# Attention and a gated two-layer network on one core: q and k of 33 head pairs turned by DMA instead of TensorE

## The chip, the core and the metric

One Trainium2 chip, one of its eight cores. The core has five engines that run side by side, each with its own queue of instructions in program order: TensorE (PE, matrix multiplications; its weight loads are shown apart as PEld), VectorE (DVE), ScalarE (ACT), GpSimd (POOL) and SyncE (SP, which here issues nearly all DMAs and does nothing else). 16 DMA engines move data between the memory of the chip (DRAM) and the core's two on-chip memories, SBUF and, for the results of TensorE, PSUM; a DMA can't reach PSUM. The metric is the time of one execution on the device, in microseconds (us).

## What is computed

```python
# q, k, v: (8, 12, 448, 64): batch, heads, sequence, head size
scale = 1.0 / np.sqrt(q.shape[-1])
scores = scale * np.matmul(q, k.transpose(0, 1, 3, 2))
m = np.max(scores, axis=-1, keepdims=True)
e = np.exp(scores - m)
attn = e / (np.sum(e, axis=-1, keepdims=True) + np.exp(-m) + 1e-09)
attn_out = np.matmul(attn, v)
x = attn_out.transpose(0, 2, 1, 3).reshape(3584, 768)
h = x @ w_in                       # (768, 2048)
g = h * np.tanh(softplus(h))       # "mish"
out = g @ w_out                    # (2048, 768)
```

Inputs and output are float32; the kernel multiplies in bfloat16.

## The kernel before, in words

The 96 heads are taken as 48 pairs, numbered by batch and then by head, six pairs a batch. A pair's two heads lie side by side on the 128 partitions. The sequence of 448 is split as 112 rows of 4.

For a pair, the steps are these. `load_pair` (L121) loads q, k and v by SP. `cast_pair` and `cast_v` (L165, L185) turn them into bfloat16 on POOL: `q_bf`, `k_bf`, `v_bf`. `transpose_pair` (L190) turns q and k on TensorE, eight transposes of 112 x 128, four for each, into a PSUM bank each (two halves of an `sc` tile in the repeating part). `evac_qk` (L221) brings them to SBUF: VectorE scales q and lays it out in `qd`, a tile with zeros in such places that one multiplication by the pair's k serves both heads (two instructions, L254, one for each head); ScalarE copies k into `kT` (L262). `scores` (L291) multiplies (L311) into one of three `sc` tiles of two PSUM banks and VectorE takes the negated row maximum (L332). `exps` (L337) has ScalarE raise the scores into `en` and sum the rows (L345). `denominators` (L363) and `normalise` (L410) have VectorE divide (seven instructions on a pair, L414) and SP turn the pair's 128 x 3584 numbers by one DMA transpose, `en` to `eT` (L422). `av_pair` (L445) multiplies by v (L462), and VectorE copies the result into `xT` (L475), the input of the network. `mm1_mish` (L493) is the first layer for 128 of the 2048 columns: six multiplications (L498), then ScalarE's Mish (L504). `mm2_part` (L523) is the second layer in small chunks (L551), with a copy by VectorE (L534) and a store by SP (L516).

The order is written out by hand. After a head part for the first batch (pairs 0 to 5), the loop at L653 runs over units of three pairs. A unit has two stretches:

- Twelve steps (L664), four for a pair: the exponentials of one step, some chunks of the second layer for an earlier batch (spread by the weights at L589), scores two steps ahead. At steps 0, 3 and 6 (`LOAD_AT`) the loads, the casts of the pair loaded one time before, and the cast of a v are issued. The pair whose cast is issued at these steps belongs to the next unit.
- Eight groups of the first layer (L724), for a batch whose attention is complete. Beside the first group stand the denominators of the unit's three pairs and the first normalisation; after groups 1, 3 and 5 the transposes and the evacuation of the next unit's three pairs; from group 4 on the first scores of the next unit.

Buffers are taken from pools in turn: `bf` with 4 tiles for each of q_bf and k_bf and 12 for v_bf, `qk` with 3 for kT. A tile that is taken again waits until its last reader is done. A DMA is also held until the DMA eight issues before it has landed, as the eight semaphores for them are used in turn.

Of the kernel before, what the change touches and what calls it, by code (L numbers as in the profile page):

```python
# [10 lines left out]
BF16 = mybir.dt.bfloat16  # L11
# [4 lines left out]
UNIT_PAIRS = 3  # L16
# [3 lines left out]
def kernel(  # L20
# [9 lines left out]
    nc = tc.nc  # L30

    B, H, S, D = q.shape
# [3 lines left out]
    NT = 4  # L36
    SP_ = S // NT
    HP = H // 2
# [9 lines left out]
    N_PAIRS = B * HP  # L48
# [4 lines left out]
    def pool(name, bufs, space=None):  # L53
        if space is None:
            return ctx.enter_context(tc.tile_pool(name=name, bufs=bufs))
        return ctx.enter_context(tc.tile_pool(name=name, bufs=bufs, space=space))
# [1 line left out]
    PS = bass.MemoryType.PSUM  # L58
    singles = pool("singles", 1)
    ld_pool = pool("ld", 3)  # L60
    bf_pool = pool("bf", 4)
    qk_pool = pool("qk", 3)
    st_pool = pool("st", 5)
    hl_pool = pool("hl", 4)
    rb_pool = pool("rb", 2)
# [38 lines left out]
    loaded, casted, qkT, att, xT, o_sbs, stats = {}, {}, {}, {}, {}, {}, {}  # L104
# [60 lines left out]
    def cast_pair(p, with_v=True):  # L165
        if p >= N_PAIRS:
            return
        q_f, k_f, v_f = (loaded[p].get(nm) for nm in "qkv")
        q_bf = bf_pool.tile([SP_, NT, 2, D], BF16, tag="q_bf", name="q_bf")
        k_bf = bf_pool.tile([SP_, NT, 2, D], BF16, tag="k_bf", name="k_bf")  # L170
        v_bf = bf_pool.tile([SP_, 2, NT * D], BF16, tag="v_bf", name="v_bf", bufs=12)
        by_t = "p h (t d) -> p t h d"
        q_t, k_t = (t.rearrange(by_t, t=NT) for t in (q_f, k_f))
        if p == 0:
            nc.vector.tensor_copy(out=k_bf, in_=k_t)
            for half in (slice(0, NT // 2), slice(NT // 2, NT)):
                nc.vector.tensor_copy(out=q_bf[:, half], in_=q_t[:, half])
        else:
            nc.gpsimd.tensor_copy(out=q_bf, in_=q_t)  # L179
            nc.gpsimd.tensor_copy(out=k_bf, in_=k_t)  # L180
        casted[p] = (q_bf, k_bf, v_bf)
        if with_v:
            cast_v(p)

    def cast_v(p):  # L185
        if p >= N_PAIRS:
            return
        nc.gpsimd.tensor_copy(out=casted[p][2], in_=loaded.pop(p)["v"])  # L188

    def transpose_pair(p, bank=None):  # L190
        if p >= N_PAIRS:
            return
        q_bf, k_bf, _ = casted[p]
        if bank is None:
            ps = mo_take()
            ps_k = mo_take() if p == 0 else ps
        else:
            ps, ps_k = sc_tiles[2 - bank][:, 0, :], sc_tiles[2 - bank][:, 1, :]
        by_s = [
            t[:, :].bitcast(BF16).rearrange("p (s n) -> p s n", s=2)[:, s, :]  # L200
            for s, t in enumerate((ps, ps_k))
        ]
        by_2 = sc_tiles[2][:, 0, :].bitcast(BF16)
        srcs = list(enumerate((q_bf, k_bf)))
        for s, src in reversed(srcs) if p == 0 else srcs:
            for t in range(NT):
                to = by_2 if p == 0 and s == 0 and t >= NT // 2 else by_s[s]
                nc.tensor.transpose(  # L208
                    to[:, t * SP_ : (t + 1) * SP_],
                    src[:, t].rearrange("p h d -> p (h d)"),  # L210
                    ident[:SP_, :SP_],
                )
        own = [] if bank is not None else [ps, ps_k] if p == 0 else [ps]
        qkT[p] = (by_s, own)
# [6 lines left out]
    def evac_qk(p, act=False):  # L221
        if p >= N_PAIRS:
            return
        (q_ps, k_ps), own = qkT[p]
        mo_free.extend(own)
        q_reads = []
        qd = q_diag[p % 3]
        kT = qk_pool.tile([128, S], BF16, tag="kT", name="kT")
        if p < DIAG_FROM:
            qT = qd.rearrange("d i h r -> d (i h r)")[:, 0:S]  # L230
            qkT[p] = (qT, kT)
            if p == 0:
                nc.scalar.copy(kT, k_ps[:, 0:S])
                by_2 = sc_tiles[2][:, 0, :].bitcast(BF16)
                for ps, half in (q_ps, slice(0, S // 2)), (by_2, slice(S // 2, S)):
                    nc.vector.tensor_scalar(
                        out=qT[:, half], in0=ps[:, half], scalar1=SCALE, scalar2=None,
                        op0=ALU.mult,
                    )
                return  # L240
            if act:
                nc.scalar.mul(qT, q_ps[:, 0:S], SCALE)
            else:
                q_reads.append(nc.vector.tensor_scalar(
                    out=qT, in0=q_ps[:, 0:S], scalar1=SCALE, scalar2=None, op0=ALU.mult
                ))
        else:
            qkT[p] = (qd, kT)
            if p < DIAG_FROM + 3:
                nc.vector.memset(qd[0:64, :, 1, :], 0.0)  # L250
                nc.vector.memset(qd[64:128, :, 0, :], 0.0)
            for h in range(2):
                rows = slice(64 * h, 64 * h + 64)
                q_reads.append(nc.vector.tensor_scalar(  # L254
                    out=qd[rows, :, h, :],
                    in0=q_ps[rows, 0:S].rearrange("d (i r) -> d i r", i=QB),
                    scalar1=SCALE, scalar2=None, op0=ALU.mult,
                ))
        if own and not act:
            nc.vector.tensor_copy(out=kT, in_=k_ps[:, 0:S])  # L260
        else:
            k_read = nc.scalar.copy(kT, k_ps[:, 0:S])  # L262
            if not own:
                apart(k_read, *q_reads)
# [145 lines left out]
    def normalise(p, dma=True):  # L410
# [9 lines left out]
        if dma:  # L420
            n = NT - 1 if p < HEAD else NT
            nc.sync.dma_start_transpose(  # L422
# [168 lines left out]
    LEAD = UNIT_PAIRS + 1  # L591
    LOAD_AT = (0, 3, 6)
    HEAD = HP

    BY_PE = {HEAD - 1: 1, HEAD: -2, HEAD + 1: 2}
    AV_AT = {0: {1: 3, 5: 4, 8: 5}, 1: {1: 8, 4: 6, 8: 7}}
# [20 lines left out]

    for p in range(HEAD):
        for s in range(STEPS):
# [33 lines left out]
    for u in range(UNITS_PER_B, N_UNITS + 2 * UNITS_PER_B):  # L653
# [10 lines left out]
        for n in range(steps):  # L664
            pi, s = divmod(n, STEPS)
            p, idx = p0 + pi, p0 * STEPS + n
            late_tp = u == UNITS_PER_B and n == STEPS
            exps(idx)
            if u == UNITS_PER_B + 1 and n == 0:
                for j in range(2):  # L670
                    turn_on_pe(HEAD, j, busy_first=3)
            flush_late()
            if late_tp:
                transpose_pair(p0 + 2)
                evac_qk(p0 + 2)
            if held and n == 1:
                late.extend(held)
                held.clear()
                flush_late()
            late.extend(slow)  # L680
            slow.clear()
            acc += weight[n]
            want = int(total * acc / sum(weight) + 1e-6)
            while done < want:
                fn, w = filler.popleft()
                fn()
                done += w
            scores_ahead(end)
            if n in LOAD_AT:
                at = p0 + LOAD_AT.index(n)  # L690
                load_pair(at + LEAD, "qk")
                load_pair(at + 1, "v")
                cast_pair(at + LEAD - 1, with_v=False)
                cast_v(at)
            for pe, n0 in BY_PE.items():
                j = n - n0
                first = 2 if pe == HEAD else 0
                if pe // UNIT_PAIRS == u - 1 < first_mm2 - 1 and first <= j < NT:
                    turn_on_pe(pe, j, busy_first=1)
            spread = RDEN_AT.get(u - UNITS_PER_B, {})  # L700
            if n in spread:
                on_act = u < first_mm2
                spread_rden(
                    spread[n], copy=nc.scalar.copy if on_act else nc.vector.tensor_copy,
                    behind=slow if on_act else late,
                )
            early = AV_AT.get(u - UNITS_PER_B)
            if early is not None and n == 7:
                keep_busy(6, bank=mo_free[0])
            if early is not None:  # L710
                if n in early:
                    av_pair(early[n], half=p)
            elif s == (2 if pi else 0) and N_PAIRS <= p < N_PAIRS + UNIT_PAIRS:
                av_pair(p - UNIT_PAIRS)
            if u - UNITS_PER_B < len(W_AT):
                at = (u - UNITS_PER_B, n)
                load_w(W_AT[at[0]].get(n, 0), behind=W_BEHIND.get(at))
# [6 lines left out]
        for f in range(FF_U):  # L724
# [19 lines left out]
            if f in (3, FF_U - 1) and p0 >= LATE_DIV:  # L744
                p = todo[1 + f // (FF_U - 1)]
# [33 lines left out]
```

## Time and profile before

| | |
|---|---|
| Time, three runs | 480.35 us in the median (479.74 to 483.63) |
| The profiled execution | 479.66 us, its span 477.9 us |
| Granted TensorE clock | 0.996 |
| Busy: PE, PEld | 458.8 us, 257.8 us |
| Busy: DVE, ACT, POOL | 358.7, 344.7, 103.8 us |
| L208, the transposes of q and k: spans of one | 213 ns, pipelined |
| L254, q scaled and laid out: 72 of them | 27.7 us, 385 ns each |
| L262, kT copied by ScalarE: 39 of them | 20.8 us, 534 ns each |
| L179 and L180, casts of q and k on POOL | 635 and 622 ns each |
| L422, DMA transposes of en: 45 of them | 6.7 us from issue to landing, in the median |
| A load of q or k, 224 KB | 5.2 us from issue to landing, in the median |

The profile is of one execution, made by the hardware's profiler. Busy time of PE counts pipelined multiplications whose spans overlap, so that the sum of single spans is more than the busy time. Times in the views are counted from the span's start. In rows of work the columns are the engine, the line of the kernel, the operation, the tile written and the tiles read, their shapes and a count. An idle time of an engine is put down to what released it, by the semaphores. SPq and POOLq are the queues that issue DMAs; the length of such a row is the time for which its engine was occupied by the issue, and the data move beside and after it. The share of the DMA engines can be more than 1, since packets that overlap on one engine are counted each.

### The profile page before, as it was taken

The page shows a single profiled execution, that of the slowest core. Times are in us where ns is not written, and L with a number is a line of the kernel's source. Part 1 is how long each engine was busy: PE and PEld are TensorE (multiplying, and loading weights), DVE is VectorE, ACT ScalarE, POOL GpSimd, SP SyncE. Part 2 cuts the span into 40 slices and gives each one's busy share as a digit, 9 for nine tenths or more (in the row PEclk, how much of TensorE's full clock was granted, in tenths as well). Part 3 has the DMA queues.
Part 4 walks back from the last instruction along what each step waited for, and adds up shares of the span by engine and source line. Part 5 has one row for each costly group of instructions (what it writes and reads, how often), then busy time and mean ns, then how long its engine had stood idle before and what let it go on. Part 6 is the DMA issues. An engine that isn't in the chain of part 4 may idle for free.

```text
span 477.9 us, 9363 instructions
## 1 busy us (share of the span) xinstructions
PE 458.8 (96%) x3291; PEld 257.8 (54%) x3291; DVE 358.7 (75%) x715; ACT 344.7 (72%) x907; POOL 103.8 (22%) x186
## 2 busy tenths in 40 slices
PE   6878999999999999999999999999999999999996
PEld 3344555555555565556555555555555555556563
DVE  5899849569898998889899979888898889421011
ACT  5998878788797868788787968687887978312300
POOL 3623536106031311304040312204040300000000
PEclk9999999999999999999999999999999999999999
DMA  8999999999999979898989999989989596961122
GB/s 215 227 224 213 234 222 183 185 212 233 195 301 207 261 149 214 211 198 227 192 229 171 267 156 260 198 192 231 190 220 198 173 181 156 156 142 34 34 63 71
DMA packets 204975, 91.09 MB, mean 191 GB/s; under 512 B 161792, under 2 KB 201472, under 8 KB 204928
## 3 DMA queue, kind: packets, MB, share of 16 engines
q1 hardware_dynamic: 197408, 84.18, 81.0%
q0 software_dynamic: 7488, 6.29, 8.8%
q8 instruction: 26, 0.43, 0.4%
q14 instruction: 21, 0.17, 0.1%
q10 hardware_dynamic: 32, 0.02, 0.0%
HBM read 45.61 MB, written 11.01 MB: 118 GB/s over the span
## 4 chain that ended last, share of the span: by engine, by line
PE 69%; DVE 8%; ACT 6%; issue 1%; DVEq 0%
PE mo L498 24%; PE mo L551 24%; PE sc L311 7%; ACT en L345 6%; PE sc L462 6%; DVE negm L332 5%; PE sc L498 3%; PE sc L208 3%; DVE en L414 1%; DVE xT L475 1%; PE mo L462 1%; DVE o_sb L534 1%; PE mo L272 0%; DVE eT L437 0%; ACT L345 0%
## 5 line engine op out<-in xcount | busy, mean ns | idle before, releaser
L345 ACT ACTIVATE en<-sc,negm 128x448 bf16<-128x448 f32 x336 | 208.7, 640 | 22.5 <-DVE negm L332 20.7
L332 DVE TENSOR_REDUCE negm<-sc 128x2 f32<-128x896 f32 x192 | 182.6, 970 | 39.6 <-PE sc L311 29.3
L551 PE MATMUL mo<-w_out_sb,gT 128*128 128x384 bf16 (+1 forms) x1024 | 166.8, 307 | 0.4 <-DVE rb L402 0.4
L498 PE MATMUL mo<-xT,w_in_sb 128*128 128x448 bf16 x672 | 141.9, 353 | 0.3 <-DVE xT L475 0.3
L551 PEld LDWEIGHTS <-gT 128*128 128x128 bf16 x1024 | 96.3, 98 | 56.0 <-issue 1.9
L504 ACT ACTIVATE gT<-mo 128x448 bf16<-128x448 f32 x112 | 59.3, 543 | 78.9 <-PE mo L498 78.6
L498 PEld LDWEIGHTS <-w_in_sb 128*128 128x128 bf16 x768 | 72.7, 98 | 63.4 <-issue 3.2
L179 POOL CAST q_bf<-q_f 112x512 bf16<-112x512 f32 x47 | 29.9, 635 | 222.1 <-DMA q_f<-in_q_dram 196.1
L414 DVE TENSOR_SCALAR en<-en,rden 128x448 bf16<-128x448 bf16 x252 | 74.2, 367 | 0.8
L311 PE MATMUL sc<-kT,qd 128*128 128x448 bf16 x252 | 71.6, 354 | 0.1
L345 ACT ACTIVATION_READ_ACCUMULATOR en<-sc,negm 128x1 f32 x336 | 71.0, 211 | 0.0
L534 DVE COPY o_sb<-mo 128x384 f32<-128x384 f32 (+1 forms) x64 | 31.8, 497 | 48.3 <-PE mo L551 48.1
L462 PE MATMUL sc<-eT,v_bf 112*64 112x448 bf16 x336 | 39.8, 357 | 1.4 <-ACT en L345 0.9
L311 PEld LDWEIGHTS <-qd 128*128 128x128 bf16 x252 | 24.4, 97 | 29.0 <-issue 12.9
L188 POOL CAST v_bf<-v_f 112x512 bf16<-112x512 f32 x48 | 29.9, 624 | 31.5 <-DMA v_f<-in_v_dram 31.4
L254 DVE TENSOR_SCALAR qd<-sc 64x448 bf16<-64x448 bf16 x72 | 27.7, 385 | 6.2 <-PE sc L208 5.4
L462 PEld LDWEIGHTS <-v_bf 112*64 112x64 bf16 x384 | 20.0, 109 | 20.0 <-issue 11.6
L180 POOL CAST k_bf<-k_f 112x512 bf16<-112x512 f32 x47 | 29.2, 622 | 6.1 <-DMA k_f<-in_k_dram 3.5
L262 ACT COPY kT<-sc 128x448 bf16<-128x448 bf16 x39 | 20.8, 534 | 0.6 <-PE sc L208 0.6
L498 PE MATMUL sc<-xT,w_in_sb 128*128 128x448 bf16 x96 | 20.8, 353 | 0.0
L475 DVE CAST xT<-sc 128x448 bf16<-128x448 f32 x33 | 20.3, 614 | 0.0
L208 PEld LDWEIGHTS <-q_bf 112*128 112x128 bf16 x192 | 13.7, 99 | 10.0 <-POOL q_bf L179 2.0
(61 smaller groups left out, 278.9 us busy)
## 6 DMA issues: line engine op xcount, KB each, us to landing
k_f<-in_k_dram SPq DMA_DIRECT2D x48, 224.0 KB, 5.2
q_f<-in_q_dram SPq DMA_DIRECT2D x48, 224.0 KB, 5.2
v_f<-in_v_dram SPq DMA_DIRECT2D x48, 224.0 KB, 5.5
w_in_sb<-in_moe_w_in_dram POOLq DMA_DIRECT2D x12, 256.0 KB, 8.7
w_out_sb<-in_moe_w_out_dram POOLq DMA_DIRECT2D x8, 384.0 KB, 10.1
out_dram<-o_sb SPq DMA_DIRECT2D x7, 336.0 KB, 3.7
out_dram<-o_sb SPq DMA_DIRECT2D x8, 288.0 KB, 4.8
out_dram<-o_sb SPq DMA_DIRECT2D x8, 240.0 KB, 3.4
```

The costliest lines, as they stand in the source:

```text
L179: nc.gpsimd.tensor_copy(out=q_bf, in_=q_t)
L180: nc.gpsimd.tensor_copy(out=k_bf, in_=k_t)
L188: nc.gpsimd.tensor_copy(out=casted[p][2], in_=loaded.pop(p)["v"])
L311: nc.tensor.matmul(sc[:, bk, 0:S], lhsT=qT[:, i].rearrange("d h r -> d (h r)"), rhs=kT, start=True, stop=True,)
L332: half_max[p] = nc.vector.tensor_reduce(out=negm, in_=sc[:, 0 : len(cols), 0:S], axis=AX.X, op=ALU.max, negate=True)
L345: e = nc.scalar.activation(out=st["en"][:, :, c, 0:SP_], in_=sc[:, bk, 0:S].rearrange("q (j c) -> q j c", j=NT), func=AF.Exp, bias=st["neg ...
L414: nc.vector.tensor_scalar(out=en[:, :, i, 0:SP_], in0=en[:, :, i, 0:SP_], scalar1=st["rden"][:, i : i + 1], scalar2=None, op0=ALU.mult,)
L462: mm = nc.tensor.matmul(av[h * 64 : (h + 1) * 64, 0:S], lhsT=v_bf[:, h, j * D : (j + 1) * D], rhs=e_h, start=(j == 0), stop=(j == NT - 1),)
L498: nc.tensor.matmul(h_ps[:, 0:S], lhsT=w_in_sb[:, dm, ff * 128 : (ff + 1) * 128], rhs=xT[b][:, dm, :], start=(dm == 0), stop=(dm == DM_T - 1),)
L504: nc.scalar.activation(out=gT[:, ff, b % 2 * S : b % 2 * S + S], in_=h_ps[:, 0:S], func=AF.Mish)
L534: nc.vector.tensor_copy(out=o_sb[:, cols.start : cols.start + n_dve], in_=st["o"][:, 0:n_dve])
L551: nc.tensor.matmul(st["o"][:, 0:n_cols], lhsT=gT[:, ff, i * 128 : (i + 1) * 128], rhs=w_out_sb[:, ff, cols], start=(ff == 0), stop=(ff == ...
```

## The change

From pair 15 on (`QK_BY_DMA_FROM = 2 * HP + UNIT_PAIRS`, 33 of the 48 pairs), q and k are no longer turned by TensorE. Right behind the issue of their casts, at steps 0, 3 and 6 of the twelve, SP issues two DMA transposes for each pair, `k_bf` to `kT` and `q_bf` to a new tile `qT`. `transpose_pair` returns without work for these pairs; `evac_qk` reads `qT` from SBUF instead of PSUM for the two instructions of VectorE, and leaves out ScalarE's copy, since kT is in place. To make room, `q_bf` and `k_bf` have 3 tiles instead of 4 and `v_bf` 8 instead of 12, taken at its cast instead of at that of q and k; `kT` has 6 instead of 3, and `qT` 3.

```diff
-    bf_pool = pool("bf", 4)
-    qk_pool = pool("qk", 3)
+    bf_pool = pool("bf", 3)
+    qk_pool = pool("qk", 6)
...
+    ahead = {}
+
+    def turn_qk_by_dma(p):
+        if not QK_BY_DMA_FROM <= p < N_PAIRS:
+            return
+        kT = qk_pool.tile([128, S], BF16, tag="kT", name="kT")
+        qT = qk_pool.tile([128, S], BF16, tag="qT", name="qT", bufs=3)
+        for to, src in (kT, casted[p][1]), (qT, casted[p][0]):
+            nc.sync.dma_start_transpose(
+                out=to.rearrange("d (t p) -> d t p", t=NT),
+                in_=src.rearrange("p t h d -> p (t h d)"),
+            )
+        ahead[p] = (qT, kT)
 
     def transpose_pair(p, bank=None):
-        if p >= N_PAIRS:
+        if p >= N_PAIRS or p in ahead:
             return
...
-        (q_ps, k_ps), own = qkT[p]
+        by_dma = p in ahead
+        (q_ps, k_ps), own = (ahead.pop(p), []) if by_dma else qkT[p]
         mo_free.extend(own)
...
-        kT = qk_pool.tile([128, S], BF16, tag="kT", name="kT")
+        kT = k_ps if by_dma else qk_pool.tile([128, S], BF16, tag="kT", name="kT")
...
+        if by_dma:
+            return
         if own and not act:
...
+    QK_BY_DMA_FROM = 2 * HP + UNIT_PAIRS
...
                 cast_pair(at + LEAD - 1, with_v=False)
+                turn_qk_by_dma(at + LEAD - 1)
                 cast_v(at)
```

More of the change, by code (lines that the diff above doesn't have):

```diff
@@ L167, in cast_pair @@
             return
-        q_f, k_f, v_f = (loaded[p].get(nm) for nm in "qkv")
+        q_f, k_f = (loaded[p][nm] for nm in "qk")
         q_bf = bf_pool.tile([SP_, NT, 2, D], BF16, tag="q_bf", name="q_bf")
         k_bf = bf_pool.tile([SP_, NT, 2, D], BF16, tag="k_bf", name="k_bf")
-        v_bf = bf_pool.tile([SP_, 2, NT * D], BF16, tag="v_bf", name="v_bf", bufs=12)
         by_t = "p h (t d) -> p t h d"
@@ L180, in cast_pair @@
             nc.gpsimd.tensor_copy(out=k_bf, in_=k_t)
-        casted[p] = (q_bf, k_bf, v_bf)
+        casted[p] = [q_bf, k_bf, None]
         if with_v:
@@ L187, in cast_v @@
             return
-        nc.gpsimd.tensor_copy(out=casted[p][2], in_=loaded.pop(p)["v"])
+        v_bf = bf_pool.tile([SP_, 2, NT * D], BF16, tag="v_bf", name="v_bf", bufs=8)
+        nc.gpsimd.tensor_copy(out=v_bf, in_=loaded.pop(p)["v"])
+        casted[p][2] = v_bf
+    ahead = {}
[10 more added lines that the diff above has]
+        ahead[p] = (qT, kT)
     def transpose_pair(p, bank=None):
-        if p >= N_PAIRS:
+        if p >= N_PAIRS or p in ahead:
             return
```

## The prediction

> **What bounds the kernel now.** I read the page first, then busy time by stretch, the timeline of one repeated stretch, and the DMA queue of SP. The page's busy line, its DMA slices and its chain:
>
> ```profile
> PE 458.8 (96%) x3291; PEld 257.8 (54%) x3291; DVE 358.7 (75%) x715; ACT 344.7 (72%) x907; POOL 103.8 (22%) x186
> ...
> DMA  8999999999999979898989999989989596961122
> ...
> PE 69%; DVE 8%; ACT 6%; issue 1%; DVEq 0%
> ```
>
> PE (TensorE) is busy 96% of the span and makes 69% of the chain. The DMA engines look nearly as full, so they need a second look below. The change works in the repeating units (three pairs each) from 113 us to 389 us. Two neighbours, in the view by stretch (length; busy us of PE, PEld, DVE, ACT, POOL; clock; DMA share; GB/s):
>
> ```profile
> 202.50:229.00 26.50, 26.40 (x182) 15.05 (x181) 23.62 (x49) 21.47 (x56) 5.62 (x9) 1.00 0.95 212
> 229.00:255.50 26.50, 26.50 (x182) 14.89 (x181) 23.42 (x49) 21.59 (x56) 5.44 (x9) 1.00 0.91 207
> ```
>
> PE is never idle in a unit of 26.5 us; DVE leaves 3, ACT 5. So PE time taken out of a unit is gained, until something else ends last. The timeline where a unit ends (start, length, engine, line, work, count):
>
> ```profile
> 246.91 3.22 DVE L414 TENSOR_SCALAR en<-en,rden 128x448 bf16<-128x448 bf16 x7
> ...
> 249.43 0.36 PE L208 MATMUL sc<-ident,q_bf 112*128 112x112 bf16 x4
> ...
> 249.63 0.36 PE L208 MATMUL sc<-ident,k_bf 112*128 112x112 bf16 x4
> ...
> 249.82 1.30 PE L498 MATMUL mo<-xT,w_in_sb 128*128 128x448 bf16 x6
> 250.05 1.60 DVE L254 TENSOR_SCALAR qd<-sc 64x448 bf16<-64x448 bf16 x4
> ...
> 250.89 0.17 PEld L311 LDWEIGHTS <-qd 128*128 128x128 bf16 x2 [0.20 <-DVE qd L254]
> 250.96 0.54 PE L311 MATMUL sc<-kT,qd 128*128 128x448 bf16 x2
> ...
> 251.69 1.81 DVE L414 TENSOR_SCALAR en<-en,rden 128x448 bf16<-128x448 bf16 x7
> ```
>
> The eight transposes of a pair take PE from 249.43 to 249.82: 0.39 us, not 8 x 213 ns, since they are pipelined. The next unit's first scores (L311, 250.96) need qd, which DVE finishes at about 250.83 after the seven multiplications of L414.
>
> **What goes.** 33 pairs (15 to 47) in 11 units. PE: 33 x 0.39 to 0.40 = 13.0 us, 1.18 a unit, on the bounding engine. The row decides this price. The Trainium skill, "TensorE: Matmul & The Clock Gate", Part 4, gives some 275 ns for one transpose inside a kernel; by that the change would take 33 x 8 x 0.275 = 73 us from PE, and the spacing here contradicts it. ACT loses 33 kT copies of 0.53 us (17.6 us), hidden: ACT waits for PE at most L504 rows there. DVE also loses its wait for the transposes (5.4 us in all at L254), which was beside PE's work.
>
> **What changes on DVE.** L254 runs 2 x 0.39 us a pair from PSUM. From SBUF the nearest row is L414, also bf16 from SBUF with 448 elements a partition: 1.81/7 = 0.26 us each when POOL is quiet, 3.22/7 = 0.46 when POOL's casts run beside it (246.91). So a pair costs 0.52 to 0.92 instead of 0.78; I take 0.52, as most L414 rows are the quick kind. That is minus 0.28 us to plus 0.14 a pair.
>
> **What comes late then.** Without two pairs' transposes PE reaches the first scores 0.79 us sooner, DVE has qd 0.28 sooner, so a unit needs 0.51 us of slack. In the 11 units the second L254 ends ahead of the first scores by 0.06, 0.84, 0.94, 1.08, 0.85, 0.13, 2.04, 1.84, 1.78, 0.76 and 1.74 us: two fall short, 0.45 + 0.38 = 0.8 us. In every other unit the fourth L498 group would ask for its bank at 247.9 while the Mish that frees it ends at 247.8 to 247.9: 0.15 x 5 = 0.7. For casts over qd I allow 1.0. Back to the gain: 13.0 - 2.5 = 10.5 us.
>
> **What is added: SP's queue.** SP issues in order. One unit of it:
>
> ```profile
> 227.20 9.56 SPq L422 DMA_TRANSPOSE eT<-en  x2
> 236.86 0.53 SPq L128 DMA_DIRECT2D q_f<-in_q_dram  x1
> ...
> 242.69 0.41 SPq L128 DMA_DIRECT2D v_f<-in_v_dram  x1
> 245.61 0.81 SPq L516 DMA_DIRECT2D out_dram<-o_sb  x2
> 250.20 8.60 SPq L422 DMA_TRANSPOSE eT<-en  x2
> ```
>
> Between the third en transpose (ends 236.8) and the next unit's first (250.20) SP issues nine loads and four stores in 7.05 us and waits 6.3; it waits 0.97 more for DVE inside the 9.56. Six new transposes a unit (kT, qT per pair) must fit into 7.3 - 1.0 (the unit gets shorter) = 6.3 us, 1.05 each with the 0.05 gap between issues: **1.0 us each is the point where SP decides**.
>
> Their price is in no row. The rows of the same kind, as min/median/max in ns:
>
> ```profile
> L422 SPq DMA_TRANSPOSE eT<-en x45: 4019/4256/17422, 13.8 to 416.9; - x45
> ```
>
> 4.25 us is for 128 x 3584 (224 tiles of 16 x 128), 4.02 the least of the first pairs' 168 tiles. The new ones have 112 x 512: 28 tiles. In proportion 4.25/8 = 0.53 us; with a plain issue (0.41, L128) as a fixed part and the rest by tiles 0.41 + 3.84/8 = 0.89; by a straight line through 168 and 224 tiles 3.4 to 3.5. None can be below nothing: each occupies SP. I take 0.9. The line is doubtful, as the 4.02 was issued behind two loads still under way (5.9 us to landing) and 7.4 and 17.4 us rows show SP held by a full queue. By 0.9, 6 x 0.95 = 5.7 us fits into 6.3; SP costs nothing, with little to spare.
>
> Which waits stand in that queue? kT of a pair waits for POOL's cast of its k. The first pair of a unit was cast a unit ago. The second was loaded one group before: cast about 5.0 us after its load's issue (237.48 to 241.9), and SP needs 1.7 + 1.9 + 0.9 + 1.6 = 6.1 to get there: no wait. The third: the same 5 to 7 us (q 239.59 to k's cast end 246.5) against 1.9 + 1.6 plus its own group 1.6: a wait of 0 to 1.9. Behind it are the stores and the en transposes. These land 6.2 us after issue (222.96 to 229.2; AV at 232.75), so 3.5 us of lateness are covered, 2.4 in the shorter unit.
>
> **The DMA engines.** A share near 1 isn't a full one:
>
> ```profile
> 225.00:228.00 3.00, 3.00 (x23) 1.76 (x22) 2.96 (x9) 1.48 (x4) 0.00 (x0) 1.00 1.16 217
> ...
> 263.00:265.00 2.00, 2.00 (x16) 0.92 (x13) 2.00 (x2) 2.00 (x7) 0.00 (x0) 1.00 1.28 291
> ```
>
> Both windows hold en transposes alone; after a hitch at 261 they ran at 291 GB/s, so 217 is SP's issue rate. A unit moves 2.75 MB of these, 2.06 of loads (310 GB/s at 243 to 245) and 0.8 of stores: 9.5 + 6.7 + 2.5 = 18.7 us; six of 0.115 MB add 2.4: 21 of 25.4. Upper bound, if the short ones use a quarter of the engines: 6 x 1.6 = 9.5, 28 us, which would bind.
>
> **Sum.** Span 477.9, profiled execution 479.66; minus 10.5 gives 469.2. The median of the runs is 0.7 above the profiled one: **470 us**.
>
> **Rivals.**
> 1. *SP becomes the bound* (slower). For: SP is in order, occupied for 19 of 26.5 us, and no row shows a short transpose below 4.02 us. Against: the two proportional readings. Above 1.0 us each, every 0.1 costs 11 x 0.6 = 6.6 us after 2.4 us of cover. At 1.2: 13.2 - 2.4 = 10.8 lost, no change. At 1.5: 33 - 2.4 = 30.6 lost, 480.35 + 20 = 500. At 3.5: 11 x 15 - 2.4 = 163 lost, 633. Chance of slower this way 0.27, of landing near no change 0.10. The Trainium skill, "VectorE: DVE Perf Modes", on the three transpose paths, speaks against the change: TensorE where PSUM will do, the DMA only otherwise, with 1309 ns a 128 x 128 block; were that an issue's price per block, 4 x 1.31 = 5.2 us. The rows (4.25 us for 28 blocks, 0.15 each) speak against that when blocks follow each other; no row shows a short one.
> 2. *DVE takes over* (no change). With casts beside both, L414 at 3.22 and qd at 0.92 in every unit, qd comes at 250.05 + 0.92 = 250.97 and PE asks at 250.17: 0.8 lost in each, 13.0 - 8.8 - 0.7 = 3.5 gained, 477. Against: five of eleven units have 1.7 us of slack. Chance 0.08.
> 3. *The DMA engines bind*: 28 us a unit, 480.35 + 11 x 1.5 = 497. Chance 0.05.
> 4. *The change doesn't do what it says*: in the built order PE has 528 instructions less (33 x 16) and SP 66 more, so this has no chance.
>
> Forecast 0.50 (gain over 1%, about 475.5). Slower by over 1% (485.2): 0.27 + 0.05 = 0.32. Within 1%, about what a measurement tells from nothing: 0.10 + 0.08 = 0.18. The range goes from 466 (all 13 us and a little of DVE's) to 500 (issue of 1.5 us); the forecast's own range is 466 to 475.
>
> **What will show it.** Right: units of 25.4 to 25.7 us with PE still full; SP rows of kT and qT at 0.5 to 1.0 us, SP waiting for DVE ahead of the first en transpose; AV never waiting. Wrong: those rows over 1.2 us and no wait of SP on DVE any more, PE idle ahead of L462's weights; or DVE's qd rows at 0.4 us and more beside casts with PE idle ahead of the scores; or kT landing late, PE idle there.

## The result, and the profile after

The change makes the kernel slower: 514.42 us in the median of six runs (512.05 to 518.57), beside 480.15 of the kernel before (479.13 to 483.63). The ratio is 1.0725, with a 95% interval of 1.0691 to 1.076. The profiled execution took 514.77 us, its span 512.9, beside 479.66 and 477.9. Where a kernel's runs lie more than 1.5% apart (e7, e14 and e18 below), its time and ratio are those of the runs within 1.5% of its fastest.

From the page of the kernel after: busy time of the engines, TensorE's granted clock in the 40 slices, and the chain.

```profile
PE 458.5 (89%) x3027; PEld 248.7 (48%) x3027; DVE 361.3 (70%) x715; ACT 332.8 (65%) x874; POOL 105.3 (21%) x186
...
PEclk8889999999799999979999899999899899999998
...
PE 56%; DMA 17%; ACT 5%; DVE 5%; issue 1%; SPq 0%; DVEq 0%
```

TensorE was busy for 96% of the span and for 69% of the chain; now for 89% and 56%. DMA, which was not in the chain, has 17% of it. The transposes did go: 264 instructions less on PE and on PEld.

One repeating unit of the kernel after, in SP's timeline (start, length, engine and queue, line, work, count). It runs from the issue of one first en transpose (L440) to the next:

```profile
244.55 13.54 SPq L440 DMA_TRANSPOSE eT<-en  x3
258.14 0.57 SPq L128 DMA_DIRECT2D q_f<-in_q_dram  x1
258.77 0.47 SPq L128 DMA_DIRECT2D k_f<-in_k_dram  x1
259.28 0.46 SPq L128 DMA_DIRECT2D v_f<-in_v_dram  x1
259.83 1.88 SPq L199 DMA_TRANSPOSE kT<-k_bf  x1
261.76 1.26 SPq L199 DMA_TRANSPOSE qT<-q_bf  x1
263.12 0.99 SPq L534 DMA_DIRECT2D out_dram<-o_sb  x2
...
271.21 1.26 SPq L199 DMA_TRANSPOSE qT<-q_bf  x1
272.57 0.99 SPq L534 DMA_DIRECT2D out_dram<-o_sb  x2
273.67 5.12 SPq L440 DMA_TRANSPOSE eT<-en  x1
```

The rows that are left out follow each other in the same way, with 0.04 to 0.11 us between them: there is no gap in the unit, where the kernel before had 7.3 us of waits. SP's sum for this unit of 29.12 us: three en transposes 13.54, nine loads 4.40, four stores 1.98, six new transposes 1.88 + 1.26 + 1.18 + 1.27 + 1.19 + 1.26 = 8.04, and 1.16 between the rows. SP has no time left, and the experiments show that this sets the unit.

The new transposes and the two instructions of VectorE that read qT, in the rows of the tiles (duration in ns, min/median/max):

```profile
L199 SPq DMA_TRANSPOSE kT<-k_bf x33: 1183/1184/2102, 105.0 to 415.5; - x33
...
L270 DVE TENSOR_SCALAR qd<-qT x66: 364/381/384, 117.0 to 420.6; 64x448 bf16<-64x448 bf16 x66
L199 SPq DMA_TRANSPOSE qT<-q_bf x33: 1247/1265/4250, 106.2 to 416.7; - x33
```

SP is held for 1.18 and 1.27 us (the medians), not 0.9. VectorE takes 0.381 us from SBUF, as it took 0.385 from PSUM. And the waits of the kernel after (us in total, times, longest):

```profile
PE sc L480 <- DMA eT<-en: 30.5, 11, 4.8
...
DVE qd L270 <- DMA qT<-q_bf: 24.3, 13, 4.4
```

SP reaches the en transposes late, eT lands late, and TensorE waits for it ahead of AV (L480), 2.8 us each time. In the kernel before, AV never waited for eT.

Two units by stretch (length; busy us of PE, PEld, DVE, ACT, POOL; granted clock; DMA share; GB/s):

```profile
215.29:244.55 29.26, 25.09 (x144) 13.15 (x142) 24.09 (x50) 18.88 (x51) 6.08 (x10) 0.88 1.03 209
244.55:273.67 29.12, 26.74 (x165) 14.52 (x164) 22.51 (x47) 21.13 (x54) 5.64 (x10) 1.00 1.09 217
```

One has a clock of 0.88, one of 1.00, and they are equally long: the lower clock is not what sets the unit.

**Where the 35 us went.** Followed by the issue of each unit's first en transpose, the kernel after is 2.0 us late at the first (119.69 beside 117.71). The next unit, the first that holds new transposes throughout, takes 36.88 us instead of 25.7: 11.2 more. The nine after it take 29.1 instead of 26.4: 24 more. The end of the run gives 2 back. So there are two losses: one in every unit, and one of 36.9 - 29.1 = 7.8 us in the first alone. That first one, in SP's timeline of the kernel after:

```profile
114.10 1.18 SPq L199 DMA_TRANSPOSE kT<-k_bf  x1
115.33 4.25 SPq L199 DMA_TRANSPOSE qT<-q_bf  x1
119.69 19.34 SPq L440 DMA_TRANSPOSE eT<-en  x3
```

The same three en transposes in the kernel before:

```profile
117.71 15.00 SPq L422 DMA_TRANSPOSE eT<-en  x3
```

GpSimd's queue then carries the last four pieces of w_out, 384 KB each, as it did before (two issued at 109.02 and two at 114.52 us; before, 110.05 and 113.23). The first unit by stretch, in the kernel after, with the columns as above:

```profile
112.00:116.00 4.00, 4.00 (x27) 2.21 (x25) 3.23 (x8) 3.95 (x10) 2.70 (x5) 1.00 1.37 153
...
128.00:132.00 4.00, 0.00 (x0) 0.00 (x0) 2.92 (x5) 1.01 (x3) 0.00 (x0) 0.93 1.24 244
132.00:136.00 4.00, 3.80 (x15) 1.67 (x16) 3.15 (x10) 2.28 (x8) 0.00 (x0) 0.50 1.11 209
```

From 112 to 116 us the share of the DMA engines is 1.37, and they move 153 GB/s; in the kernel before it is 1.26 in this stretch, and they move 218. The first of the three en transposes alone holds SP for 10.21 us and lands 12.4 us after its issue. TensorE has nothing to do from 127.4 to 132.2 us, waiting 4.8 us for that eT, and then gets half its clock for four. The clock is not what makes this unit long: SP is occupied without a pause from 119.69 to 156.57 us.

### The profile page after: what moved, and what is told of

Its sections match the earlier page's. It is cut to its first block, busy times and chain, and to the rows that moved or that the text cites. A ratio compares the mean times of both kernels' runs of the same rounds, so it can differ in the third digit from the quotient of the medians.

```text
span 512.9 us, 8876 instructions
## 1 busy us (share of the span) xinstructions
PE 458.5 (89%) x3027; PEld 248.7 (48%) x3027; DVE 361.3 (70%) x715; ACT 332.8 (65%) x874; POOL 105.3 (21%) x186
## 4 chain that ended last, share of the span: by engine, by line
PE 56%; DMA 17%; ACT 5%; DVE 5%; issue 1%; SPq 0%; DVEq 0%
PE mo L516 21%; PE mo L569 16%; DMA eT<-en 16%; PE sc L329 7%; PE sc L480 7%; ACT en L363 5%; DVE negm L350 4%; PE sc L516 3%; DMA qT<-q_bf 1%; PE mo L480 1%; PE mo L290 0%; DVE xT L493 0%; DMA out_dram<-o_sb 0%; DVE o_sb L552 0%; DVE eT L455 0%
## 5 line engine op out<-in xcount | busy, mean ns | idle before, releaser
L569 PE MATMUL mo<-w_out_sb,gT 128*128 128x384 bf16 (+1 forms) x1024 | 171.8, 312 | 1.4 <-DMA w_out_sb<-in_moe_w_out_dram 1.0
L516 PE MATMUL mo<-xT,w_in_sb 128*128 128x448 bf16 x672 | 138.2, 353 | 0.3 <-DVE xT L493 0.3
L569 PEld LDWEIGHTS <-gT 128*128 128x128 bf16 x1024 | 97.9, 99 | 60.7 <-issue 8.9
L516 PEld LDWEIGHTS <-w_in_sb 128*128 128x128 bf16 x768 | 74.3, 98 | 69.5 <-issue 3.5
L432 DVE TENSOR_SCALAR en<-en,rden 128x448 bf16<-128x448 bf16 x252 | 77.1, 377 | 0.9
L480 PE MATMUL sc<-eT,v_bf 112*64 112x448 bf16 x336 | 42.8, 377 | 36.3 <-DMA eT<-en 30.5
L329 PE MATMUL sc<-kT,qd 128*128 128x448 bf16 x252 | 74.4, 366 | 0.0
L480 PEld LDWEIGHTS <-v_bf 112*64 112x64 bf16 x384 | 21.4, 112 | 55.9 <-issue 49.1
L270 DVE TENSOR_SCALAR qd<-qT 64x448 bf16<-64x448 bf16 x66 | 24.9, 377 | 24.8 <-DMA qT<-q_bf 24.3
L516 PE MATMUL sc<-xT,w_in_sb 128*128 128x448 bf16 x96 | 20.8, 353 | 0.0
```

The source lines that it names most:

```text
L329: nc.tensor.matmul(sc[:, bk, 0:S], lhsT=qT[:, i].rearrange("d h r -> d (h r)"), rhs=kT, start=True, stop=True,)
L432: nc.vector.tensor_scalar(out=en[:, :, i, 0:SP_], in0=en[:, :, i, 0:SP_], scalar1=st["rden"][:, i : i + 1], scalar2=None, op0=ALU.mult,)
L480: mm = nc.tensor.matmul(av[h * 64 : (h + 1) * 64, 0:S], lhsT=v_bf[:, h, j * D : (j + 1) * D], rhs=e_h, start=(j == 0), stop=(j == NT - 1),)
L516: nc.tensor.matmul(h_ps[:, 0:S], lhsT=w_in_sb[:, dm, ff * 128 : (ff + 1) * 128], rhs=xT[b][:, dm, :], start=(dm == 0), stop=(dm == DM_T - 1),)
L569: nc.tensor.matmul(st["o"][:, 0:n_cols], lhsT=gT[:, ff, i * 128 : (i + 1) * 128], rhs=w_out_sb[:, ff, cols], start=(ff == 0), stop=(ff == ...
```

## The experiments

In all of them time is that of 1 core in us, and a ratio is to the kernel before on the same chip. Unit lengths are taken from the timeline of SP, from first en transpose to first en transpose: the first unit, and the mean of the nine behind it. Where new transposes start at pair 18, the first unit is still the one from some 117 us on, and the first of them are issued in it, behind its en transposes.

| kernel | first unit | mean of the next nine | median time | ratio, 95% interval |
|---|---|---|---|---|
| before | 25.7 | 26.4 | 480.15 | 1 |
| after | 36.9 | 29.1 | 514.42 | 1.0725 (1.0691 to 1.076) |
| e1_both | 35.0 | 29.3 | 516.21 | 1.0754 (1.0723 to 1.0785) |
| e2_no_turn | 29.8 | 25.5 | 474.15 | 0.9878 (0.9829 to 0.9927) |
| e3_from18 | 31.3 | 29.2 | 506.45 | 1.0551 (1.052 to 1.0582) |
| e4_one_dma | 32.6 | 26.6 | 484.33 | 1.009 (1.0061 to 1.0119) |
| e8_one18 | 26.9 | 26.4 | 480.41 | 1.0 (0.9972 to 1.0029) |
| e13_unit18 | 30.9 | 28.8 | 505.72 | 1.0524 (1.046 to 1.0588) |
| e15_late18 | 28.2 | 28.6 | 504.08 | 1.0496 (1.0474 to 1.0519) |
| e16_two18 | 25.9 | 25.9 | 476.24 | 0.9927 (0.9911 to 0.9944) |
| e17_two_late18 | 25.8 | 26.6 | 483.35 | 1.0061 (1.0039 to 1.0082) |
| e7_pool18 | 43.4 | 31.1 | 539.58 | 1.126 (1.1196 to 1.1324) |
| e18_before_pool | 40.7 | 35.5 | 577.10 | 1.2025 (1.1997 to 1.2053) |

### Is it SP, or what is turned and read?

**e1_both**: TensorE turns q and k as before, and the DMA transposes are issued as well, into tiles that nobody reads.

```diff
-        kT = qk_pool.tile([128, S], BF16, tag="kT", name="kT")
+        kT = qk_pool.tile([128, S], BF16, tag="jk", name="jk")
...
-        ahead[p] = (qT, kT)
```

> TensorE turns q and k of all pairs as before, and from pair 15 on SP issues the same 66 DMA transposes of the changed kernel as well, into tiles that nobody reads. Theory S (SP's queue is the bound: 29.2 us of issues in a unit, never idle): the unit stays at about 29.2 us although nothing waits for a turned tile, 508 to 518 us. Rival L (the tiles land late, and VectorE waits for qT, 24.3 us): nobody waits here, 479 to 486 us. Rival E (the 16 DMA engines have too much to move) expects 508 to 518 like S; the third and fourth run and those of a later call tell the two apart.

516.21, within the 508 to 518 expected: as slow as the change itself, although nothing waits for kT or qT as the DMA writes them. The waits of this kernel:

```profile
PE sc L479 <- DMA eT<-en: 26.0, 15, 4.9
```

So it is not that kT and qT land late: the 36 us, with no saving of TensorE's in them, are there when the new transposes only stand in SP's queue, ahead of the en transposes.

**e2_no_turn**: the opposite. From pair 18 on nothing is turned at all; the pairs read the kT and qT of pairs 15 to 17. This leaves the turning of 30 pairs out of the computation.

```diff
-        kT = qk_pool.tile([128, S], BF16, tag="kT", name="kT")
-        qT = qk_pool.tile([128, S], BF16, tag="qT", name="qT", bufs=3)
+        qT, kT = once[p % 3]
+        ahead[p] = (qT, kT)
+        if p >= QK_BY_DMA_FROM + 3:
+            return
```

> Leaves out the turning of q and k after pair 17: all later pairs compute with the q and k of pairs 15 to 17, which are turned once by DMA. All else is as in the changed kernel, so it shows what TensorE's relief alone is worth. If the prediction's gain of 10.5 us was right in itself: 467 to 473 us, units of 25.4 to 25.7 us. If VectorE or ScalarE would have taken it anyway: 477 to 481.

Units of 25.5 us, inside the 25.4 to 25.7 of the prediction, with qd read from SBUF at 0.38 us each. TensorE's share of the forecast holds. The time, 474.15, is 1.15 above the 467 to 473 expected: the first unit, with six DMA transposes ahead of it, is 4.1 us longer than before; without that it would be some 470, an estimate. The buffers are as small here as in the change, so they don't make its loss either.

### Is it the number of issues, or the bytes?

**e4_one_dma**: q and k of a pair lie in one tile, and one transpose of 112 x 1024 (56 tiles of 16 x 128) turns both. The bytes are the same, the packets 0.4% fewer, the issues half.

```diff
+        qk_bf = bf_pool.tile([SP_, 2, NT, 2, D], BF16, tag="qk_bf", name="qk_bf")
+        q_bf, k_bf = qk_bf[:, 0], qk_bf[:, 1]
...
-        for to, src in (kT, casted[p][1]), (qT, casted[p][0]):
-            nc.sync.dma_start_transpose(
...
+        nc.sync.dma_start_transpose(
+            out=qkT2.rearrange("d x (t p) -> d (x t) p", t=NT),
+            in_=both.pop(p).rearrange("p x t h d -> p (x t h d)"),
+        )
```

> q and k of a pair are cast into one tile and turned by one DMA transpose of 112 x 1024 (56 tiles of 16 x 128) instead of two of 28. Buffers are cut to fit (v 6). Bytes and packets on the DMA engines stay the same. Theory S with a fixed part in the price (a line through 28 tiles at 1.22 us and 224 at 4.25 gives 1.65 us for 56): three such issues save 2.5 us of SP in a unit, the unit falls to 26.5 to 27 us, 480 to 492 us in all. Rival E (DMA engines): 510 to 518 us. If the price has no fixed part but goes by tiles or rows: 2.4 us for one, 508 to 516 us.

484.33, 30 us better than the change, and within the 480 to 492 expected of a price with a fixed part. The row of the turned tile in this kernel:

```profile
L199 SPq DMA_TRANSPOSE qkT<-qk_bf x33: 1221/1234/2082, 104.9 to 386.2; - x33
```

56 tiles hold SP for 1.23 us, 28 tiles for 1.18 to 1.27. Up to there the price is per issue, and SP's queue is what set the unit. Since the bytes are the same and the packets nearly so, the DMA engines are not the bound.

### The first unit

**e3_from18**: the change from pair 18 on, a unit later, when the weights have arrived. **e8_one18**: the same with one transpose a pair.

```diff
-    QK_BY_DMA_FROM = 2 * HP + UNIT_PAIRS
+    QK_BY_DMA_FROM = 2 * HP + 2 * UNIT_PAIRS
```

> As the changed kernel, but the DMA turns from pair 18 on, so that the first unit with DMA transposes comes after the last loads of weights. Theory S alone, 2.4 to 3.2 us for each unit: 511 us. With theory W beside it (in the first unit the weights' packets on GpSimd's queue slow the transposes: the step from 119.7 to 156.6 us took 11 us more than before): 498 to 504 us.

> One DMA transpose for q and k of a pair, from pair 18 on. The steady unit of the run from pair 15 was 26.5 us, as before the change; with theory W its loss of 4 us against before lay in the first unit, so 479 to 482 us. Without theory W: 483 to 485 us.

e3 lies between its two expectations, 2.5 us above the one with the weights. It is 8.0 us quicker than the change: by SP's price alone a unit less gives back 29.1 - 26.4 = 2.7, so some 5 are the first unit's own. The three en transposes of its first unit hold SP for 15.13 us, as in the kernel before (15.00), not 19.34. e8, as expected, is 3.9 quicker than e4, and its first unit 26.9 instead of 32.6. So the first unit's loss ends when the new transposes start a unit later. That it is a collision with the weights is argued, not shown: they are what is under way on another queue there and nowhere later, but no run moves the weights themselves.

### Another queue beside the transposes

**e7_pool18** was meant to free SP: from 18 on with two transposes a pair, and the loads of q, k and v of later units issued by GpSimd. **e18_before_pool** does this move alone in the kernel before, where nothing but en is turned by DMA.

```diff
+    by_pool = [False]
...
-            nc.sync.dma_start(
+            (nc.gpsimd if by_pool[0] else nc.sync).dma_start(
...
+        by_pool[0] = u > first_mm2
```

> Two DMA transposes for each pair as in the changed kernel, from pair 18 on; the loads of q, k and v of the later units are issued by GpSimd instead of SP. Bytes on the DMA engines stay the same, SP loses nine issues of a unit (4.8 us). Theory S: SP's sum falls from 29.2 to 24.4 us, under TensorE's 25.5 (the unit that the run without turning had), so units of 25.4 to 25.8 us and 469 to 473 us. Rival E (the DMA engines bound): units stay at 29 us, 500 to 508 us. If packets of the loads, now on a queue of their own, slow the transposes as the weights' did: SP rows of en over 5 us, 475 to 495 us.

> The kernel before with the loads of q, k and v of units from the second batch's second on issued by GpSimd instead of SP; nothing is turned by DMA but en. W (packets of another queue in flight stretch SP's transposes, the en transposes too): their rows at 5 us and more, units of 28 to 36 us, 500 to 530 us. N (it takes the short transposes, or SP's length, to make the loss seen with the loads on the other queue): SP loses 4.9 us a unit that it had to spare, units of 26.5, 478 to 483 us.

e7 missed all three of its expectations, the nearest by over 30 us; only the sign of the third, rows of en over 5 us, came. Its row of the en transposes (min/median/max in ns):

```profile
L442 SPq DMA_TRANSPOSE eT<-en x45: 3931/5208/17269, 13.3 to 474.8; - x45
```

The median is 5.2 us instead of 4.3. e18 shows the loss without any new transpose, and more of it than expected: 577 us instead of 500 to 530, with units of 35.5, within the expected 28 to 36. Its row, TensorE's wait for eT, and one unit in SP's timeline:

```profile
L424 SPq DMA_TRANSPOSE eT<-en x45: 3845/5652/18247, 13.6 to 514.2; - x45
...
PE sc L464 <- DMA eT<-en: 69.8, 18, 9.1
```

```profile
226.53 26.35 SPq L424 DMA_TRANSPOSE eT<-en  x3
252.94 7.91 SPq L518 DMA_DIRECT2D out_dram<-o_sb  x4
265.66 24.34 SPq L424 DMA_TRANSPOSE eT<-en  x3
```

SP has only the en transposes and the stores left, and yet three en transposes take 20 to 26 us in the eight units behind the first, instead of 13.5 to 15.0, and all of them land 11.4 us after issue in the median instead of 6.7. In the last two units, when no loads are left to issue, they take 14.9 and 13.5 again. The loads have the same bytes as before, but three things change with their queue. In SP's queue they were issued behind one unit's en transposes and ahead of the next one's; on their own queue they are issued when GpSimd's casts let them, and that is beside the en transposes. The queue itself is another, of the kind that the page of the profile calls software_dynamic. And the packets are larger: 90 loads make 21600 packets less on SP's queue and 7200 more on GpSimd's, so a load of 229376 bytes goes in 80 packets of some 2.9 KB instead of 240 of some 1 KB.

The Trainium skill, "DMA: Bandwidth & Descriptors", Queues, rings and completion order, says that each DMA engine serves its queues in turn, a packet at a time. With a transpose's packets, which the page of the profile counts under 512 bytes (31680 more in the kernel after than before, 480 for each of 66), against the loads' larger ones, that could give what is seen here, if the profile's packets are those that the skill means. But no run varies the packets' size alone, or the time of issue alone, so which of the three it is stays open. The same page of the Trainium skill, in Issuing engines are not separate DMA queues, holds that issuing from several engines saves only issue time; here the kernel with the loads on GpSimd's queue took 20% longer.

### Can SP be freed otherwise?

**e13_unit18**: one transpose of 168 tiles for the three pairs of a unit, from 18 on, issued behind the third pair's casts.

```diff
-        if not QK_BY_DMA_FROM <= p < N_PAIRS:
+        if not QK_BY_DMA_FROM <= p < N_PAIRS or p % UNIT_PAIRS != UNIT_PAIRS - 1:
             return
...
+            out=to.rearrange("d u x (t p) -> d (u x t) p", t=NT),
+            in_=unit_bf.rearrange("p u x t h d -> p (u x t h d)"),
```

> One DMA transpose for q and k of all three pairs of a unit (112 x 3072, 168 tiles), from pair 18 on; the loads stay on SP. Bytes as in the changed kernel. The two runs with 28 and 56 tiles showed the same issue time, 1.2 us. Theory S, with 168 tiles at 1.2 us (if the time is fixed) to 3.3 us (by a line from 56 to 224): SP's sum falls to 22 to 24.3 us, TensorE bounds with 25.5, 469 to 473 us in all. Rival E: 500 to 508 us.

505.72, a miss of the 469 to 473; it lies in the range for the DMA engines as the bound, but e8 moves the same bytes in 480.41. In its rows, the transpose, VectorE's wait for what it writes, and SP's own wait ahead of it for the last casts:

```profile
L205 SPq DMA_TRANSPOSE qkT<-unit_bf x10: 3172/3873/4144, 142.2 to 402.0; - x10
```

```profile
DVE qd L277 <- DMA qkT<-unit_bf: 32.4, 10, 4.2
...
SPq L205 <- POOL v_bf L187: 32.0, 10, 5.5
```

168 tiles hold SP for 3.87 us, no less than three times 1.23: joining more than 56 tiles saves nothing. And nothing is turned before the last cast: SP waits 3.2 us for it in every unit, and VectorE another 3.2 for what lands, with TensorE's scores behind it.

**e14_unit18_pool** is e13 with the loads on GpSimd's queue.

> Both: one DMA transpose for a unit and the loads on GpSimd's queue, from pair 18 on. Theory S: TensorE is the bound in either, so no gain over the better of the two: 469 to 473 us. If the SP queue still cost something in the one before, up to 2 us less.

559.2 us, far from the 469 to 473 expected. e13's loss of 25.6 us and e7's of 59.5 would make 85, where 79 came; how the two add up is not shown.

**e15_late18**: e8, with each transpose issued one load group later, so that SP doesn't wait for casts. In e8 those waits cost it 18.3 us in 16 times:

```profile
SPq L199 <- POOL v_bf L190: 18.3, 16, 3.5
```

```diff
-                turn_qk_by_dma(at + LEAD - 1)
+                if n:
+                    turn_qk_by_dma(at + LEAD - 2)
...
+            if f == 1:
+                turn_qk_by_dma(nxt + 2)
```

> One transpose a pair from pair 18 on, each issued one load group later (the first pair's behind the second group's loads, the second's behind the third group's, the third's behind the first en transpose), so that its casts are done when SP comes to it. S (SP's occupied time alone sets the unit): without the 1.3 us that SP waits for casts in each unit, its sum is 13.9 + 4.9 + 2.1 + 3 x 1.28 = 24.8 us, under TensorE's 25.5; units of 25.5 us, 470 to 474 us. C (what is left is the collision of transfers, which stretches rows and lands them late whatever their place): units stay at 26.4, 478 to 482; the third pair's transpose between the en transposes would then show as a wait of the AV matmuls for eT.

504.08, outside both expectations: 24 us slower than e8 by its order alone. VectorE in one unit of e15 (idle time before a row, and what ended it, in brackets):

```profile
258.62 2.35 DVE L432 TENSOR_SCALAR en<-en,rden 128x448 bf16<-128x448 bf16 x7
...
263.52 0.78 DVE L270 TENSOR_SCALAR qd<-qkT 64x448 bf16<-64x448 bf16 x2 [1.87 <-DMA qkT<-qk_bf]
264.32 1.81 DVE L432 TENSOR_SCALAR en<-en,rden 128x448 bf16<-128x448 bf16 x7
...
269.19 0.77 DVE L270 TENSOR_SCALAR qd<-qkT 64x448 bf16<-64x448 bf16 x2 [2.06 <-DMA qkT<-qk_bf]
```

A ring of two queues: VectorE's qd waits for a transpose that lands late; behind qd stands the multiplication of the next en (L432); SP's next en transpose waits for that; and behind it stands the next unit's work of SP. Over the run qd waits 44.6 us in 23 times. SP had been freed at one end and tied at the other.

**e16_two18**: e8 with only the first two pairs of a unit turned by DMA, the third by TensorE. **e17_two_late18**: the same with both a load group later.

```diff
-        if not QK_BY_DMA_FROM <= p < N_PAIRS:
+        if not QK_BY_DMA_FROM <= p < N_PAIRS or p % UNIT_PAIRS == UNIT_PAIRS - 1:
             return
```

> As the version with one transpose a pair from pair 18 on, but the third pair of each unit is turned by TensorE. S: SP is 1.3 us freer in each unit and the wait for the third pair's casts is gone, 23.5 to 24.5 us of SP; TensorE gets 0.39 back and needs 25.9: 473 to 476 us. C: 478 to 482.

> Two pairs of each unit by one transpose each from pair 18 on, each issued one load group later; the third by TensorE. S: SP's sum 13.9 + 4.9 + 2.1 + 2.6 = 23.5 us without a wait, TensorE 25.9: 473 to 476 us, no quicker than the one with three if that reaches 471. C: 478 to 482.

e16 takes 476.24 us (473 to 476 were expected), 0.7% less than the kernel before, and is the quickest of those that do the whole computation. Its units are 25.9 us, as expected of TensorE, and its page shows the chain without DMA again:

```profile
PE 453.9 (96%) x3131; PEld 249.8 (53%) x3131; DVE 361.8 (77%) x715; ACT 337.1 (71%) x887; POOL 104.5 (22%) x186
...
PE 56%; DVE 17%; ACT 9%; issue 1%; DVEq 0%
```

SP has gaps again, as here ahead of the first en transpose, 2.6 us:

```profile
269.92 0.49 SPq L129 DMA_DIRECT2D v_f<-in_v_dram  x1
273.02 4.47 SPq L440 DMA_TRANSPOSE eT<-en  x1
```

e17 has the same issues, is 7 us slower, and misses both of its expectations (473 to 476, 478 to 482). qd waits for its DMA again (in e16 it never does):

```profile
DVE qd L270 <- DMA qkT<-qk_bf: 15.4, 10, 2.9
```

So there are two limits: SP's sum, and the time by which a pair must be turned. Of the two orders tried, that of the change, each transpose right behind its casts, is the better one.

## Why the prediction was wrong

**The step that failed is the price of one issue, "I take 0.9".** It was interpolated between a plain issue and a large transpose, with a part that goes by tiles. The rows show 1.18 and 1.27 us at 28 tiles and 1.23 at 56: a floor, which no row of the kernel before could show, since all its transposes had 168 tiles or more. With that, the first rival's condition was met, and e1, e2 and e4 show that it is this rival: the loss stays when nothing reads the result, goes when nothing is issued, and nearly goes when half as many issues move the same bytes. The first of the signs that the prediction named for being wrong is what the profile shows: rows of some 1.2 us, and TensorE idle ahead of AV.

**Rival 1 had the right mechanism and three wrong sizes**; at 1.2 us it gave no change, where 514 was measured. From its own formula:

- The price. With the rows that are stretched (1.88 and 2.10 us appear) and the gaps, six cost 8.04 us in the unit shown, 1.34 each, and 0.3 for the gaps behind them, as the prediction counted them. (1.34 - 1.0) x 66 - 2.4 of cover = 20 us lost.
- The point from which SP decides. The 7.3 us of waits were read in a unit of 27.2 us and used as if for one of 26.5. SP is occupied for 27.2 - 7.3 = 19.9, which leaves 5.6 of 25.5, and 0.88 a transpose instead of 1.0: 66 x 0.12 = 8 us.
- The en transposes, taken as unchanged. Behind the short ones the first of a unit takes 5 us (4.97 and 5.12 in the rows), 13.5 for three instead of 12.8: 0.7 x 10 = 7 us.
- The first unit, not foreseen at all: 7.8 us.

479.7 - 10.5 + 20 + 8 + 7 + 7.8 = 512, where the profiled execution took 514.8. That it comes so close is luck: the split is an estimate from one unit, but its parts are in rows.

**What held.** TensorE's gain of 10.5 us in 11 units, 0.95 a unit: e2's units are 25.5 us instead of 26.4. That the DMA engines, whose share was near 1, are not the bound: e4 moves the same bytes in 30 us less. That the third pair's transpose would wait in SP's queue for its casts: it does in e8, where SP comes early enough; in the change itself SP was late anyhow (4.1 us of such waits in all).

**What was off without a cost.** qd from SBUF was taken at 0.26 us by the row of L414 and takes 0.38, 66 x 0.12 = 8 us of VectorE; e2 has it and still makes the predicted unit. Rival 2's price beside casts, 0.46, never came: the longest of the 66 rows is 0.384. The 0.28 us by which qd was to come sooner is 0.26 by the prediction's own rows, which changes nothing. ScalarE did lose the 17.6 us of copies (20.8 to 3.2), and no run shows a gain from that.

**What was missing.** That the weights would still be under way on another queue when the first short transposes start (that they make the first unit's loss is argued above, not shown). The prediction followed the queue of SP and the engines' share, and did not ask what else is under way on another queue. In the steady units, too, some rows of the new transposes are stretched where they run behind loads; what does that was not tried.

## What to carry to other kernels

A DMA transpose costs its issuing queue a floor, here 1.2 us up to 56 tiles and some 0.02 us a tile beyond it: count issues before bytes, join what is ready together, and stop before the queue's time is used up, as e16 does with two pairs of three. Before work goes to an in-order queue, add up everything that it issues in one period and compare that with the shortened period, over an average one; then follow each new wait to what stands behind it in both queues. And a transfer that is moved from a queue to relieve it is issued at another time and in other packets: here the loads on another queue beside transposes cost 97 us (e18), far more than the issue time that was saved.

## What the runs showed of the hardware

- How long one DMA transpose holds SP, in the median: 1.18 to 1.27 us for 28 tiles, 1.23 for 56, 3.87 for 168 (3.17 to 4.14), 4.3 for 224.
- With the loads issued on GpSimd's queue while they run, three en transposes hold SP for 20 to 26 us instead of 13.5 to 15.0, with the same bytes (e18, whose time is 1.20 times as long); in its units without loads they take 14.9 and 13.5.
- VectorE's scaling of bf16 takes 0.381 us from SBUF and 0.385 from PSUM with this layout (64 partitions, a strided write), while L432's, on 128 partitions and as many elements in each, follow each other at 0.26 (seven in 1.81 us).
- After 4.8 us in which TensorE did nothing (127.4 to 132.2 us of the kernel after) the granted clock was 0.50 from 132 to 136 us and 0.72 in the next four. The Trainium skill, "TensorE: Matmul & The Clock Gate", Part 1, tells of half the rate after an idle window of some 3.4 us, and the trace agrees. Here it followed the loss and did not make it, as SP's row without a pause shows.
